# A fused attention and PReLU kernel: relu split by load counters, and the side tasks of a group gathered in one slot

## The chip, the cores and the metric

The kernel runs on one core of a Trainium2 chip. The metric is the device time of one execution in microseconds (us). Five engines work side by side and meet only at semaphores: TensorE (PE, with weight loads listed apart as PEld), VectorE (DVE), ScalarE (ACT), GpSimd (POOL) and SyncE (SP); the last two mostly issue DMAs here. TensorE writes its results into PSUM, which has eight banks of 512 float32 columns over 128 partitions; ACT and DVE read them from there.

## The reference

Four batches of x (12480 rows of 128) go through two attention steps with 32 inducing rows, and the result through a dense layer pair with a PReLU between:

```python
h = mab(I, x)          # 32 rows attend to the 12480 rows of x
a = mab(x, h)          # the 12480 rows of x attend to the 32 rows of h
t = a @ w_in                                   # 128 -> 2048
g = np.maximum(t, 0.0) + alpha * np.minimum(t, 0.0)
out = g @ w_out                                # 2048 -> 128
```

`mab(q, kv)` is softmax(q kv^T / sqrt(128)) kv. The output is 49920 by 128 float32.

## The kernel before

**What is computed how.** The second attention's weights are kept unnormalised: e2 = exp(scores), 32 values for a row of x. Since a @ w_in = (e2 @ h @ w_in) / sum(e2), the kernel makes hW = h @ w_in once for a batch and multiplies e2 with it; the division is done at the very end (it may be moved past the relu, since the sum is positive). PReLU is written as (1 - alpha) relu(t) + alpha t: the first term goes through relu and W1 = (1 - alpha) w_out, the second is linear and folds into a small matrix hA = h @ (w_in diag(alpha) w_out), which is added by "bias matmuls" from e2.

**Tiles.** A group is 512 rows of x (the last group of a batch 192), a supergroup is four groups; a batch has 25 groups. A group is worked in four slots j = 0 to 3. So there are 4 x 25 x 4 = 400 slots, and a flat loop over them (L622 to L630) fixes the order of all engines. A helper `pin` (L56) chains each instruction to the one before it on its engine, so the order written is the order run.

**A slot.** `fill` (L385) issues four matmuls of 32 x 128 weights over 512 columns. The four use different rows of the array, and e2 stands four times over the partitions (`rep`, a replica, made by a trip to DRAM). Each fills one PSUM bank of a ring of six (`bank`, L93). Then each bank is emptied by one relu with a cast to bf16 into the tile gt: on ACT (L405) or on DVE (L408). After the fill come the tasks of this slot, if any, and then `mm2` (L413) of the slot before: 16 matmuls of 128 x 128 that multiply gt with W1 and add into an accumulator (two PSUM banks, taken in turn by groups). After a group's last slot DVE multiplies the accumulator with 1/sum(e2) (`ob`, L441), and POOL issues the DMA to the output.

So in TensorE's order, slot n is: fill n, tasks of n, output matmuls of n - 1. I call the four banks of a fill r = 0 to 3, and write a slot's engines as a word: AADA means that ACT empties banks 0, 1 and 3, and DVE bank 2. As the ring has six banks and a fill takes four, a fill needs the banks that the last fill's r = 0 and 1 used; each task between them takes one bank more and moves that need on by one.

**Who empties a bank.** Before, a small planner decides. It keeps three clocks (TensorE, ACT, DVE; L90) and a time at which each bank comes free; every step adds its estimated time with `spent` (L99), the exponentials, reciprocals and ob among them. In `fill` a bank goes to the engine that would end first (L402, L403). The estimates are in the lines L397 and L398.

**Bias matmuls.** Four matmuls from `rep` with hA (L427 to L434) are added to the accumulator by the `mm2` of j = 0 (for the first group of all by that of j = 3).

**Tasks.** While a batch runs, TensorE also prepares what follows: for the next supergroup the scores (`b_scores`, L306, one exponential on ACT), its replicas by DMA (`b_rep`, L327) and the denominators (`b_den`, L360, sixteen columns and a reciprocal on DVE); for the next batch the load (`a_load`, on POOL's queue), a transposing DMA (`a_xpose`, on SP's), the scores (`a_scores`, with an exponential on ACT and a transposing DMA), the accumulation (`a_accum`, with an addition on DVE), and at its end six steps that make h, hW and hA (`h_sum` to `h_linear`). The lines L592 to L620 place them by group and slot with `at(group, function, j)`; j is 1 where none is given. The supergroup's scores, replicas and denominators stand at j = 3 of three groups in a row, the next batch's steps at j = 1, and the h steps at j = 1 and j = 3.

**Head.** L551 to L574, and the tasks of the first group, prepare batch 0 on TensorE itself, as it has nothing else to do then; POOL scales the weights in eight operations (`w_scale`, L516).

Of the kernel before, what the change touches and what calls it, by code (L numbers as in the profile page):

```python
# [15 lines left out]
P = 128  # L16
NB = 4
GRP = P * NB
NQ = 4
# [5 lines left out]
def kernel(  # L25
# [59 lines left out]
    accs = [psum.tile([P, NB, C], f32, name=f"acc{i}") for i in range(2)]  # L85
    ring_n = [0]

    clk = {"P": 0.0, "A": 0.0, "D": 0.0}  # L90
    free = [0.0] * RING

    def bank():  # L93
        i = ring_n[0] % RING
        ring_n[0] += 1
        clk["P"] = max(clk["P"], free[i])
        return ring[i]

    def spent(e, ns, release=True):  # L99
        clk[e] = max(clk[e], clk["P"] + 100) + ns  # L100
        if release:
            free[(ring_n[0] - 1) % RING] = clk[e] + 100

    def mm(o, lhsT, rhs, start=True, stop=True, **kw):
        return pin(nc.tensor.matmul(o, lhsT, rhs, start=start, stop=stop, **kw))  # L105
# [5 lines left out]
    def new_batch(b):  # L111
        st = Batch()
        st.b = b
        st.xT = xt_pool.tile([C, NS, NQ, GRP], bf16, name="xT", tag="xT")
        st.xTr = xt_pool.tile([C, JR, PR], bf16, name="xTr", tag="xTr")
        st.xn = {}
        st.e1 = {}
        st.e1T = {}
        st.es = work.tile([P, NS + 1], f32, name="es", tag="es")
        st.hacc = work.tile([P, C], f32, name="hacc", tag="hacc")  # L120
        st.e2 = {}
        st.d = {}
        st.rep = {}
        st.rden = {}
        nc.vector.memset(st.es[:], 0.0)
        nc.vector.memset(st.hacc[:], 0.0)
        return st
# [80 lines left out]
    def a_scores(st, u, by_dma=True):  # L208
        ps = bank()
        if u < NS:  # L210
            for q in range(NQ):
                mm(ps[32 * q : 32 * q + 32, :], IT[:], st.xT[:, u, q, :])
            e1 = work.tile([P, GRP], bf16, name="e1", tag="e1")
            pin(nc.scalar.activation(
                out=e1[:], in_=ps[:], func=EXP, scale=scale, accum_out=st.es[:, u : u + 1]
            ))
            if by_dma:
                e1T = work.tile([P, NB, P], bf16, name="e1T", tag="e1T")
                pin(nc.sync.dma_start_transpose(out=e1T[:], in_=e1[:]))
        else:  # L220
            mm(ps[0:M, :REM], IT[:], st.xTr[:].rearrange("c j p -> c (j p)"))
            e1 = e1r
            pin(nc.scalar.activation(
                out=e1[:, :, :PR],
                in_=ps[0:M, :REM].rearrange("m (j p) -> m j p", j=JR),
                func=EXP, scale=scale, accum_out=st.es[0:M, u : u + 1],
            ))
            if by_dma:
                e1T = work.tile([P, JR, M], bf16, name="e1Tr", tag="e1Tr")
                pin(nc.sync.dma_start_transpose(  # L230
                    out=e1T[:], in_=e1[:].rearrange("m j p -> m (j p)")
                ))
        clk["P"] += 320
        spent("A", 680)
        if by_dma:
            st.e1T[u] = e1T
        else:
            st.e1[u] = e1

    def a_accum(st, u):  # L240
        xn = st.xn.pop(u)
        e1T = st.e1T.pop(u)
        ps = bank()
        clk["P"] += 240
        if u < NS:
            for j in range(NB):
                for q in range(NQ):
                    mm(
                        ps[32 * q : 32 * q + 32, :C],
                        e1T[:, j, 32 * q : 32 * q + 32],  # L250
                        xn[:, q, j * C : (j + 1) * C],
                        start=(j == 0), stop=(j == NB - 1),
                    )
            pin(nc.vector.tensor_tensor(
                out=st.hacc[:], in0=ps[:, :C], in1=st.hacc[:], op=ADD
            ))
        else:
            for j in range(JR):
                mm(
                    ps[0:M, :C], e1T[:PR, j, :], xn[:, j, :],  # L260
                    start=(j == 0), stop=(j == JR - 1),
                )
            pin(nc.vector.tensor_tensor(
                out=st.hacc[0:M, :], in0=ps[0:M, :C], in1=st.hacc[0:M, :], op=ADD
            ))

        spent("D", 220)

    def h_sum(st):
        st.et = work.tile([P, 1], f32, name="et", tag="et")  # L270
# [35 lines left out]
    def b_scores(st, s):  # L306
        ps = bank()
        if s < NS:
            for q in range(NQ):
                mm(ps[32 * q : 32 * q + 32, :], st.hT, st.xT[:, s, q, :])  # L310
            e2 = work.tile([P, GRP], bf16, name="e2", tag="e2")
            pin(nc.scalar.activation(out=e2[:], in_=ps[:], func=EXP, scale=scale))
            w = GRP
        else:
            mm(ps[0:M, :REM], st.hT, st.xTr[:].rearrange("c j p -> c (j p)"))
            e2 = work.tile([M, REM], bf16, name="e2r", tag="e2r")
            pin(nc.scalar.activation(out=e2[:], in_=ps[0:M, :REM], func=EXP, scale=scale))
            w = REM

        nq = NQ if s < NS else 1  # L320
        st.d[s] = dram.tile([32 * nq, w], bf16, name="e2d", tag="e2d" if s < NS else "e2dr")
        pin(nc.sync.dma_start(out=st.d[s][:], in_=e2[:]))
        clk["P"] += 320
        spent("A", 490)
        st.e2[s] = e2

    def b_rep(st, s):  # L327
        nq, w = (NQ, GRP) if s < NS else (1, REM)
        rep = rep_pool.tile([P, nq, w], bf16, name="rep", tag="rep" if s < NS else "repr")
        dv = st.d.pop(s)[:].rearrange("(q i) t -> i q t", q=nq)  # L330
        for r in range(4):
            pin(nc.sync.dma_start(out=rep[32 * r : 32 * r + 32], in_=dv))
        for q in range(nq):
            st.rep[s * NQ + q] = rep[:, q, :]


    def b_scores_pe(st, s, q):
# [22 lines left out]
    def b_den(st, s):  # L360
        e2 = st.e2.pop(s)
        ps = bank()
        clk["P"] += 240
        spent("D", 250)
        if s < NS:
            for j in range(NB):
                mm(ps[:, j * NQ : (j + 1) * NQ], e2[:, j * P : (j + 1) * P], pick[:])
# [11 lines left out]
        st.rden[s] = rd  # L379


    def shape_of(g):
        return (P, NB) if g < NS * NQ else (PR, JR)

    def fill(st, g, j):  # L385
# [5 lines left out]
        for r in range(4):  # L391
# [1 line left out]
            mm(  # L393
                ps[:, :w], st.hW[32 * r : 32 * r + 32, j, :], rep[32 * r : 32 * r + 32, :w]
            )
            banks.append((ps, (ring_n[0] - 1) % RING))
        ca, cd = w * 0.75 + 96, w * 1.04 + 68  # L397
        clk["P"] += 100 + w * 0.42  # L398
        ready = clk["P"] + 50
        done = ready  # L400
        for r, (ps, i) in enumerate(banks):
            ta, td = max(clk["A"], ready) + ca, max(clk["D"], ready) + cd  # L402
            if ta <= td:  # L403
                clk["A"] = free[i] = ta
                pin(nc.scalar.activation(out=gt[:, r, :w], in_=ps[:, :w], func=RELU))  # L405
            else:
                clk["D"] = free[i] = td
                pin(nc.vector.tensor_relu(gt[:, r, :w], ps[:, :w]))  # L408
            free[i] += 150
            done = max(done, free[i])  # L410
        return gt, done

    def mm2(st, g, j, gt, done):  # L413
        pp, nb = shape_of(g)
        acc = accs[(st.b * NG + g) % 2]
        clk["P"] = max(clk["P"], done) + 4 * nb * 57
        for r in range(4):
            c = r * NJ + j
            for k in range(nb):
# [2 lines left out]
                    start=(j == 0 and r == 0 and k == 0), stop=False,  # L422
                    skip_group_check=True,
                )


        if j == (NJ - 1 if (st.b, g) == (0, 0) else 0):  # L427
            clk["P"] += nb * 57
            rep = st.rep[g]
            for k in range(nb):  # L430
                mm(
                    acc[:pp, k, :], rep[:, k * pp : (k + 1) * pp], st.hA[:],
                    start=False, stop=True, skip_group_check=True,
                )  # L434
        if j == NJ - 1:
            s, q = divmod(g, NQ)
            rd = st.rden[s]
            rq = rd[:, :, q : q + 1]
# [2 lines left out]
            pin(nc.vector.tensor_tensor(  # L441
                out=ob[:pp, :nb, :], in0=acc[:pp, :nb, :], in1=rbc, op=MULT
            ))
            spent("D", nb * C * 1.04 + 68, release=False)
            t0 = st.b * N + g * GRP
            pin(nc.gpsimd.dma_start(  # L446
                out=out[t0 : t0 + pp * nb, :].rearrange("(p j) c -> p j c", j=nb),
# [144 lines left out]
    for b in range(B):  # L592
        base = b * NG
        for s in range(1, NS + 1):
            g = base + s * NQ - 4
            at(g, lambda b=b, s=s: b_scores(states[b], s), 3)
            at(g + 1, lambda b=b, s=s: b_rep(states[b], s), 3)
            at(g + 2, lambda b=b, s=s: b_den(states[b], s), 3)
        if b + 1 < B:
            n = b + 1  # L600

# [4 lines left out]
            for i, u in enumerate(order):  # L606
                k = base + i * (NG - 13) // NS
                at(k, lambda n=n, u=u: a_load(states[n], u))
                at(k + 3, lambda n=n, u=u: a_xpose(states[n], u))
                at(k + 5, lambda n=n, u=u: a_scores(states[n], u))  # L610
                at(k + 8, lambda n=n, u=u: a_accum(states[n], u))
            k = base + NG - 5
            at(k, lambda n=n: h_sum(states[n]))
            at(k, lambda n=n: h_den(states[n]), 3)
            at(k + 1, lambda n=n: h_transpose(states[n]))
            at(k + 1, lambda n=n: h_weights(states[n]), 3)
            at(k + 2, lambda n=n: b_scores(states[n], 0))
            at(k + 2, lambda n=n: h_linear(states[n]), 3)
            at(k + 3, lambda n=n: b_rep(states[n], 0), 0)
            at(k + 3, lambda n=n: b_den(states[n], 0))  # L620

    prev = None  # L622
    for b, g, j in fills:
        gt, done = fill(states[b], g, j)
        for fn in tasks.pop((b * NG + g, j), []):
            fn()
        if prev is not None:
            mm2(*prev)
        prev = (states[b], g, j, gt, done)
    mm2(*prev)  # L630
    assert not tasks, tasks

# [29 lines left out]
```

## Time and profile before

| what | value |
|---|---|
| median of three runs | 626.52 us (626.24 to 626.53) |
| the profiled execution | 626.24 us, of which the span of the trace is 624.4 us |
| TensorE, matmuls | busy 602.7 us, 97% of the span |
| TensorE, weight loads | busy 446.3 us, 71% |
| DVE, ACT, POOL | busy 84%, 81%, 14% |
| granted TensorE clock | 0.996 of full speed, mean over the span |
| relus of 512 columns | ACT some 0.59 us each, DVE some 0.68 us |

The profile is of one execution. Its span reaches from the first to the last instruction. A line of the timeline gives an instruction's start, its duration, its engine, the line of the kernel, the operation, what it writes and reads, and how often it stands there in a row; in brackets the engine's idle time before it, and what ended it. Matmuls overlap and their ends are modelled, so the sum of their busy times can fill a span in which TensorE could still do more. In the page's name for a tile, ring_81 to ring_86 are the six ring banks, and acc_87 and acc_88 the two accumulators.

### The profile page before, as it was taken

To read this page: it belongs to the slowest core of one execution; us is meant where nothing else is said; L and a number is where in the kernel's file an instruction comes from. 1 tells how busy PE (TensorE), PEld (TensorE's weight loads), DVE (VectorE), ACT (ScalarE), POOL (GpSimd) and SP (SyncE) were. 2 spreads that over 40 slices of the span, in tenths; PEclk is the share of its full clock that TensorE was granted. 3 is DMA by queue.
4 is the path that set the end of the run, shared out by engine and by line. 5 is a ranking of instruction groups with operands and counts; after the bars stand their busy time and mean duration, and the time that the engine had idled before them with its cause. 6 is when DMAs were issued, how large, how long until landed. Compare 5 with 4: busy or idle time off the path is not lost.

```text
span 624.4 us, 21883 instructions
## 1 busy us (share of the span) xinstructions
PE 602.7 (97%) x9198; PEld 446.3 (71%) x9198; DVE 523.5 (84%) x933; ACT 507.4 (81%) x995; POOL 89.4 (14%) x152
## 2 busy tenths in 40 slices
PE   5889999999999999999999999999999999999994
PEld 3557777777777777777777777777777777777773
DVE  4568888888988888888888888888898988898893
ACT  2568888888878888888888888888888888888883
POOL 7131111110111121110111111110111011101110
PEclk9999999999999999999999999999999999999998
DMA  8723889833124488863123588854121222122111
GB/s 138 172 65 71 157 176 180 177 89 94 56 86 116 111 182 168 162 159 89 57 77 90 116 175 163 177 148 121 60 81 58 79 94 76 55 93 95 53 40 41
DMA packets 87394, 68.66 MB, mean 110 GB/s; under 512 B 53200, under 2 KB 80640, under 8 KB 87296
## 3 DMA queue, kind: packets, MB, share of 16 engines
q0 software_dynamic: 21504, 39.92, 26.2%
q1 hardware_dynamic: 65792, 27.35, 19.7%
q8 instruction: 72, 1.18, 0.8%
q14 instruction: 26, 0.21, 0.1%
HBM read 39.94 MB, written 28.62 MB: 110 GB/s over the span
## 4 chain that ended last, share of the span: by engine, by line
PE 58%; issue 32%; POOL 3%; ACT 1%; DVE 1%; POOLq 0%; DVEq 0%; ACTq 0%
PE acc_87 L105 20%; PE acc_88 L105 20%; POOL out_dram L446 3%; PE ring_81 L105 3%; PE ring_83 L105 3%; PE ring_85 L105 3%; PE ring_84 L105 3%; PE ring_86 L105 3%; PE ring_82 L105 3%; DVE gt L408 0%; ACT gt L405 0%; PE acc_88 L528 0%; ACT rep L342 0%; ACT winT L537 0%; POOL xn L136 0%
## 5 line engine op out<-in xcount | busy, mean ns | idle before, releaser
L105 PEld LDWEIGHTS <-gt 128*128 128x128 bf16 x6272 | 352.7, 98 | 83.3 <-issue 78.6
L105 PE MATMUL acc_87<-W_173,gt 128*128 128x128 bf16 (+1 forms) x3136 | 209.8, 220 | 0.0
L105 PE MATMUL acc_88<-W_173,gt 128*128 128x128 bf16 (+1 forms) x3136 | 209.7, 220 | 0.0
L446 POOL DMA_DIRECT2D out_dram<-ob x100 | 54.1, 541 | 509.8 <-DVE ob L441 490.4
L105 PE MATMUL ring_86<-rep,hW 32*128 32x512 bf16 (+1 forms) x274 | 103.5, 378 | 0.5 <-ACT rep L342 0.5
L105 PE MATMUL ring_81<-rep,hW 32*128 32x512 bf16 (+1 forms) x274 | 104.0, 380 | 0.0
L405 ACT ACTIVATE gt<-ring_85 128x512 bf16<-128x512 f32 (+1 forms) x163 | 94.3, 578 | 11.5 <-ACT gt L405 8.4
L405 ACT ACTIVATE gt<-ring_81 128x512 bf16<-128x512 f32 (+1 forms) x150 | 87.3, 582 | 19.3 <-ACT gt L405 15.0
L105 PE MATMUL ring_84<-rep,hW 32*128 32x512 bf16 (+1 forms) x272 | 102.9, 378 | 0.0
L405 ACT ACTIVATE gt<-ring_83 128x512 bf16<-128x512 f32 (+1 forms) x156 | 89.8, 576 | 15.9 <-ACT gt L405 9.0
L105 PE MATMUL ring_83<-rep,hW 32*128 32x512 bf16 (+1 forms) x267 | 100.8, 378 | 0.1
L408 DVE TENSOR_SCALAR gt<-ring_84 128x512 bf16<-128x512 f32 (+1 forms) x138 | 90.6, 656 | 12.2 <-ACT gt L405 5.6
L105 PE MATMUL ring_85<-rep,hW 32*128 32x512 bf16 (+1 forms) x259 | 97.9, 378 | 0.0
L408 DVE TENSOR_SCALAR gt<-ring_81 128x512 bf16<-128x512 f32 x124 | 85.0, 686 | 15.3 <-PE ring_83 L105 8.1
L405 ACT ACTIVATE gt<-ring_82 128x512 bf16<-128x512 f32 x149 | 88.2, 592 | 10.8 <-ACT gt L405 8.3
L405 ACT ACTIVATE gt<-ring_84 128x512 bf16<-128x512 f32 x134 | 80.0, 597 | 20.7 <-ACT gt L405 12.6
L408 DVE TENSOR_SCALAR gt<-ring_86 128x512 bf16<-128x512 f32 (+1 forms) x127 | 83.7, 659 | 15.6 <-PE ring_82 L105 10.1
L105 PE MATMUL ring_82<-rep,hW 32*128 32x512 bf16 (+1 forms) x254 | 96.2, 379 | 0.0
L405 ACT ACTIVATE gt<-ring_86 128x512 bf16<-128x512 f32 x147 | 87.3, 594 | 10.7 <-ACT gt L405 7.0
L408 DVE TENSOR_SCALAR gt<-ring_83 128x512 bf16<-128x512 f32 x111 | 75.9, 684 | 10.7 <-ACT gt L405 5.5
L408 DVE TENSOR_SCALAR gt<-ring_82 128x512 bf16<-128x512 f32 (+1 forms) x105 | 70.1, 667 | 10.5 <-PE ring_84 L105 3.7
L408 DVE TENSOR_SCALAR gt<-ring_85 128x512 bf16<-128x512 f32 x96 | 66.0, 687 | 8.6 <-PE ring_81 L105 3.0
(301 smaller groups left out, 391.2 us busy)
## 6 DMA issues: line engine op xcount, KB each, us to landing
out_dram<-ob POOLq DMA_DIRECT2D x96, 256.0 KB, 2.6
rep<-e2d SPq DMA_DIRECT2D x92, 128.0 KB, 3.4
xn<-in_x_dram POOLq DMA_DIRECT2D x18, 512.0 KB, 6.0
xn<-in_x_dram POOLq DMA_DIRECT2D x12, 256.0 KB, 8.5
w_out_f<-in_moe_w_out_dram POOLq DMA_DIRECT2D x1, 1024.0 KB, 13.6
w_in_b<-in_moe_w_in_dram POOLq DMA_DIRECT2D x1, 512.0 KB, 11.6
out_dram<-ob POOLq DMA_DIRECT2D x4, 96.0 KB, 2.0
xT<-xn SPq DMA_TRANSPOSE x18, 4.6
```

The source lines that it names most:

```text
L105: return pin(nc.tensor.matmul(o, lhsT, rhs, start=start, stop=stop, **kw))
L405: pin(nc.scalar.activation(out=gt[:, r, :w], in_=ps[:, :w], func=RELU))
L408: pin(nc.vector.tensor_relu(gt[:, r, :w], ps[:, :w]))
L446: pin(nc.gpsimd.dma_start(out=out[t0 : t0 + pp * nb, :].rearrange("(p j) c -> p j c", j=nb), in_=ob[:pp, :nb, :],))
```

## The change

The change is named "head pipelined one supergroup deeper, weight scaling in 8 wide gpsimd operations, filler transposes in TensorE gaps, softmax sums folded into the h transpose". The two files agree in the code for all of that: L551 to L574, `w_scale`, `warm` and the h steps themselves stand in both. What differs is this:

- The planner with its clocks is gone. Two counters take its place, one for ACT and one for DVE, of relu time given out so far; ob counts on DVE's, the exponentials, reciprocals and other steps on neither. A bank goes to the engine whose counter would be lower. Bank 3 of j = 0 always goes to ACT.
- The bias matmuls are issued by the `mm2` of j = 3 in all groups.
- All tasks stand at j = 1. A supergroup's scores move from j = 3 of one group to j = 1 of the next; its replica DMAs are issued in the same step as the scores' store to DRAM; its denominators move from j = 3 to j = 1 of the same group.
- The next batch's steps come 2, 4 and 6 groups after the load, in place of 3, 5 and 8, and the h steps begin two groups earlier.

```diff
@@ fill @@
-        ca, cd = w * 0.75 + 96, w * 1.04 + 68
-        clk["P"] += 100 + w * 0.42
-        ready = clk["P"] + 50
...
-            ta, td = max(clk["A"], ready) + ca, max(clk["D"], ready) + cd
-            if ta <= td:
-                clk["A"] = free[i] = ta
...
+        ca, cd = w / 1.2 + 98, w / 0.96 + 75
+        for r in range(4):
+            on_act = load["A"] + ca <= load["D"] + cd
+            if j == 0 and r == 3:
+                on_act = True
+            if on_act:
+                load["A"] += ca
...
+            else:
+                load["D"] += cd
@@ mm2 @@
-        if j == (NJ - 1 if (st.b, g) == (0, 0) else 0):
+        if j == NJ - 1:
             rep = st.rep[g]
             for k in range(nb):
...
-            spent("D", nb * C * 1.04 + 68, release=False)
+            load["D"] += pp * nb / 0.96 * (pp / P) + 75
@@ tasks @@
-            at(g, lambda b=b, s=s: b_scores(states[b], s), 3)
-            at(g + 1, lambda b=b, s=s: b_rep(states[b], s), 3)
-            at(g + 2, lambda b=b, s=s: b_den(states[b], s), 3)
+            at(g + 1, lambda b=b, s=s: b_scores(states[b], s))
+            at(g + 2, lambda b=b, s=s: b_den(states[b], s))
...
-                at(k + 3, lambda n=n, u=u: a_xpose(states[n], u))
-                at(k + 5, lambda n=n, u=u: a_scores(states[n], u))
-                at(k + 8, lambda n=n, u=u: a_accum(states[n], u))
-            k = base + NG - 5
+                at(k + 2, lambda n=n, u=u: a_xpose(states[n], u))
+                at(k + 4, lambda n=n, u=u: a_scores(states[n], u))
+                at(k + 6, lambda n=n, u=u: a_accum(states[n], u))
+            k = base + NG - 7
             at(k, lambda n=n: h_sum(states[n]))
-            at(k, lambda n=n: h_den(states[n]), 3)
-            at(k + 1, lambda n=n: h_transpose(states[n]))
-            at(k + 1, lambda n=n: h_weights(states[n]), 3)
-            at(k + 2, lambda n=n: b_scores(states[n], 0))
-            at(k + 2, lambda n=n: h_linear(states[n]), 3)
-            at(k + 3, lambda n=n: b_rep(states[n], 0), 0)
-            at(k + 3, lambda n=n: b_den(states[n], 0))
+            at(k + 1, lambda n=n: h_den(states[n]))
+            at(k + 2, lambda n=n: h_transpose(states[n]))
+            at(k + 3, lambda n=n: h_weights(states[n]))
+            at(k + 3, lambda n=n: b_scores(states[n], 0))
+            at(k + 3, lambda n=n: h_linear(states[n]))
+            at(k + 4, lambda n=n: b_den(states[n], 0))
```

More of the change, by code (lines that the diff above doesn't have):

```diff
@@ L86 @@
     ring_n = [0]
-    clk = {"P": 0.0, "A": 0.0, "D": 0.0}
-    free = [0.0] * RING
     def bank():
-        i = ring_n[0] % RING
+        t = ring[ring_n[0] % RING]
         ring_n[0] += 1
[L96 to L102, printed above, removed]
+        return t
     def mm(o, lhsT, rhs, start=True, stop=True, **kw):
@@ L121, in new_batch @@
         st.e2 = {}
-        st.d = {}
         st.rep = {}
@@ L232, in a_scores @@
                 ))
-        clk["P"] += 320
-        spent("A", 680)
         if by_dma:
@@ L243, in a_accum @@
         ps = bank()
-        clk["P"] += 240
         if u < NS:
@@ L265, in a_accum @@
             ))
-        spent("D", 220)
     def h_sum(st):
@@ L320, in b_scores @@
         nq = NQ if s < NS else 1
[L321 to L328, printed above, removed]
+        d = dram.tile([32 * nq, w], bf16, name="e2d", tag="e2d" if s < NS else "e2dr")
+        pin(nc.sync.dma_start(out=d[:], in_=e2[:]))
         rep = rep_pool.tile([P, nq, w], bf16, name="rep", tag="rep" if s < NS else "repr")
-        dv = st.d.pop(s)[:].rearrange("(q i) t -> i q t", q=nq)
+        dv = d[:].rearrange("(q i) t -> i q t", q=nq)
         for r in range(4):
@@ L334, in b_rep @@
             st.rep[s * NQ + q] = rep[:, q, :]
+        st.e2[s] = e2
     def b_scores_pe(st, s, q):
@@ L362, in b_den @@
         ps = bank()
-        clk["P"] += 240
-        spent("D", 250)
         if s < NS:
@@ L379, in b_den @@
         st.rden[s] = rd
+    load = {"A": 0.0, "D": 0.0}
     def shape_of(g):
@@ L395, in fill, with mm2 @@
             )
-            banks.append((ps, (ring_n[0] - 1) % RING))
-        ca, cd = w * 0.75 + 96, w * 1.04 + 68
-        clk["P"] += 100 + w * 0.42
-        ready = clk["P"] + 50
-        done = ready
-        for r, (ps, i) in enumerate(banks):
-            ta, td = max(clk["A"], ready) + ca, max(clk["D"], ready) + cd
-            if ta <= td:
-                clk["A"] = free[i] = ta
-                pin(nc.scalar.activation(out=gt[:, r, :w], in_=ps[:, :w], func=RELU))
-            else:
[L407 to L413, printed above, removed]
+            banks.append(ps)
+        ca, cd = w / 1.2 + 98, w / 0.96 + 75
[5 more added lines that the diff above has]
+                load["A"] += ca
+                pin(nc.scalar.activation(out=gt[:, r, :w], in_=banks[r][:, :w], func=RELU))
+            else:
+                load["D"] += cd
+                pin(nc.vector.tensor_relu(gt[:, r, :w], banks[r][:, :w]))
+        return gt
+    def mm2(st, g, j, gt):
         pp, nb = shape_of(g)
         acc = accs[(st.b * NG + g) % 2]
-        clk["P"] = max(clk["P"], done) + 4 * nb * 57
         for r in range(4):
@@ L424, in mm2 @@
                 )
-        if j == (NJ - 1 if (st.b, g) == (0, 0) else 0):
-            clk["P"] += nb * 57
+        if j == NJ - 1:
             rep = st.rep[g]
@@ L434, in mm2 @@
                 )
-        if j == NJ - 1:
             s, q = divmod(g, NQ)
@@ L608 @@
                 at(k, lambda n=n, u=u: a_load(states[n], u))
-                at(k + 3, lambda n=n, u=u: a_xpose(states[n], u))
-                at(k + 5, lambda n=n, u=u: a_scores(states[n], u))
-                at(k + 8, lambda n=n, u=u: a_accum(states[n], u))
-            k = base + NG - 5
+                at(k + 2, lambda n=n, u=u: a_xpose(states[n], u))
+                at(k + 4, lambda n=n, u=u: a_scores(states[n], u))
+                at(k + 6, lambda n=n, u=u: a_accum(states[n], u))
+            k = base + NG - 7
             at(k, lambda n=n: h_sum(states[n]))
-            at(k, lambda n=n: h_den(states[n]), 3)
-            at(k + 1, lambda n=n: h_transpose(states[n]))
-            at(k + 1, lambda n=n: h_weights(states[n]), 3)
-            at(k + 2, lambda n=n: b_scores(states[n], 0))
-            at(k + 2, lambda n=n: h_linear(states[n]), 3)
-            at(k + 3, lambda n=n: b_rep(states[n], 0), 0)
-            at(k + 3, lambda n=n: b_den(states[n], 0))
+            at(k + 1, lambda n=n: h_den(states[n]))
[4 more added lines that the diff above has]
+            at(k + 4, lambda n=n: b_den(states[n], 0))
     prev = None
     for b, g, j in fills:
-        gt, done = fill(states[b], g, j)
+        gt = fill(states[b], g, j)
         for fn in tasks.pop((b * NG + g, j), []):
@@ L628 @@
             mm2(*prev)
-        prev = (states[b], g, j, gt, done)
+        prev = (states[b], g, j, gt)
     mm2(*prev)
```

## The prediction

> **What bounds the kernel now.** I read the page first: busy shares, then the chain that ended last.
>
> ```profile
> PE 602.7 (97%) x9198; PEld 446.3 (71%) x9198; DVE 523.5 (84%) x933; ACT 507.4 (81%) x995; POOL 89.4 (14%) x152
> ...
> PE 58%; issue 32%; POOL 3%; ACT 1%; DVE 1%; POOLq 0%; DVEq 0%; ACTq 0%
> ```
>
> The chain is TensorE (58%) and TensorE that waits for nothing the profile shows (32%); ACT and DVE, which empty its PSUM banks, hold 1% each. The table of windows, for the stretch in which the 400 slots run (columns: length, then busy us and instruction counts of PE, PEld, DVE, ACT, POOL, then clock and DMA), says the same:
>
> ```profile
> 45.00:610.00 565.00, 564.93 (x8657) 419.13 (x8654) 495.30 (x846) 481.44 (x945) 67.38 (x118) 1.00 0.47 111
> ```
>
> Since ends of matmuls are modelled, I trust starts only: the distance between two fills' first weight loads (LDWEIGHTS <-hW) in the timeline. A slot without a task takes 1.32 to 1.33 us; with the four bias matmuls 1.55 (so +0.22); with those and a scores or accumulate task 1.88 (+0.33); with a denominator task 1.43 (+0.10). These numbers return for every slot of a kind: TensorE runs at its own pace, and that pace is the floor. It is left in two kinds of slot, and both show how this kernel loses time. Here is a denominator slot (j = 3), from the timeline:
>
> ```profile
> 75.02 0.10 PEld L105 LDWEIGHTS <-hW 32*128 32x128 bf16 x4
> ...
> 75.35 0.25 PE L105 MATMUL ring_83<-pick,e_1127 128*128 128x4 bf16 x4
> ...
> 75.49 0.60 ACT L405 ACTIVATE gt<-ring_85 128x512 bf16<-128x512 f32 x1 [0.27 <-ACT gt L405]
> 75.53 0.69 DVE L408 TENSOR_SCALAR gt<-ring_86 128x512 bf16<-128x512 f32 x1
> 75.98 0.59 ACT L405 ACTIVATE gt<-ring_81 128x512 bf16<-128x512 f32 x1
> 76.14 0.68 DVE L408 TENSOR_SCALAR gt<-ring_82 128x512 bf16<-128x512 f32 x1
> 76.44 0.10 PEld L105 LDWEIGHTS <-hW 32*128 32x128 bf16 x4
> 76.45 0.38 PE L105 MATMUL ring_84<-rep,hW 32*128 32x512 bf16 x1
> ...
> 76.63 0.37 PE L105 MATMUL ring_81<-rep,hW 32*128 32x512 bf16 x1
> ```
>
> The task took a bank (ring_83), so the next fill needs ring_81, the third bank of this one, in place of only the first two. ACT frees it at 75.98 + 0.59 = 76.57; the matmul starts 0.06 later, 0.18 after its sisters, and the slot that should take 1.33 takes 1.48: 19 such slots, 0.15 each. The other kind is the slot after the output multiply (ob), where two banks in a row are ACT's:
>
> ```profile
> 60.30 0.68 DVE L408 TENSOR_SCALAR gt<-ring_84 128x512 bf16<-128x512 f32 x1
> 60.50 0.10 PEld L105 LDWEIGHTS <-hW 32*128 32x128 bf16 x4
> ...
> 60.89 0.68 DVE L441 TENSOR_TENSOR ob<-acc_88,rd 128x512 f32<-128x512 f32 x1
> 60.97 0.60 ACT L405 ACTIVATE gt<-ring_85 128x512 bf16<-128x512 f32 x1 [0.24 <-ACT gt L405]
> 61.47 0.59 ACT L405 ACTIVATE gt<-ring_86 128x512 bf16<-128x512 f32 x1
> 61.49 0.68 DVE L408 TENSOR_SCALAR gt<-ring_81 128x512 bf16<-128x512 f32 x1
> ...
> 62.11 0.37 PE L105 MATMUL ring_86<-rep,hW 32*128 32x512 bf16 x1
> ```
>
> ob holds DVE from 60.89, so DVE gets one bank of this slot, the third, which nobody needs soon. ACT's second release lands 1.61 after the fill's start; the slot is 1.55 long because the bias matmuls are in it (j = 0's matmuls run one slot late), and the loss is 0.03 (38 slots of 1.35 to 1.37). So before loses 19 x 0.15 + 38 x 0.03 = 4.0 us in banks.
>
> **The rule I use.** Times from a fill's start: first relu 0.47; ACT's next 0.50 later, DVE's 0.61 later; a relu lasts 0.60 on ACT, 0.68 on DVE; hand-over 0.05. Releases: first 1.12 (ACT) or 1.20 (DVE), ACT's second 1.62, third 2.12, DVE's second 1.81. A fill without tasks before it needs the first two banks of the last fill, with one task the first three, with two all four. A wait costs release minus slot length minus 0.03 (1.61 - 1.43 - 0.03 = 0.15, as measured). Behind a waiting fill stand TensorE's 16 output matmuls, and ob behind those: a wait is paid in full.
>
> **What does not move.** The words of the change name the head, the weight scaling, filler transposes and the folded sums; all four stand alike in both files, so they cost nothing. TensorE's instructions are equal in number and kind. DVE loses 12 relus to ACT (899 becomes 911 of 1600), neither being the bound: nothing. The replica DMAs now follow the scores' store at once on SP's queue, where they wait for it and hold back the transposes behind them. They did so before too, for SP waits on data and not on slots (a store at 40.94, its first copy at 42.68); only their place among the transposes changes. Store and copies take 1.7 + 3.4 us (the latter the page's median to landing); the transposes have two groups (11 us) before a matmul needs them, the replica 2.7 groups (15 us): nothing. If that cover went, TensorE would wait up to a landing, 3.4 us, at each of 24 supergroups, 80 us; with three times the time in hand I leave that out of the range.
>
> **What moves: the bias matmuls go from j = 0 to j = 3.** Their 0.22 now lengthens the slot ahead of ob's slot, not ob's slot itself. So group slot 0 is 1.55 long, and DVE's order there is relus, ob, relus of slot 1. The accumulator is ready 0.11 after slot 1's fill starts (ob at 43.60 after a fill at 43.49); with two DVE relus before it, ob starts at 0.47 + 2 x 0.61 - 1.55 = 0.13. The next DVE relu starts 0.60 later, at 0.73, and frees its bank at 0.73 + 0.68 + 0.05 = 1.46; DVE's second at 2.07. The old planner knew this and gave slot 1 the pattern AADA (94 of 100). The counters know only totals: slot 1 is ADAD, DADA, DAAD or ADAA in 82 cases of the 99 after the first group, and DVE owns one of the first two banks.
>
> **What moves: all tasks go to j = 1**, the very slot in which DVE is late. Prices by slot 1's tasks (pattern counts are read off the changed program's order of instructions):
> - none, 33 slots, next fill wanted at 1.36: DVE first 24 x 0.10 = 2.4; AADA or AAAD 8 x (1.61 - 1.36) = 2.0; one DDAA 0.71. Sum 5.1.
> - one scores task, 24 slots, third bank wanted at 1.69: only DADA waits, 9 x (2.07 - 1.69) = 3.4. Six slots with an h step alike: 2 x 0.4 = 0.8.
> - denominator alone, 9 slots, third bank at 1.46: DADA 5 x 0.61 = 3.1; the rest 4 x 0.15 = 0.6. Sum 3.7.
> - several tasks, 27 slots: two denominators 3 x 0.53; denominator and accumulate 3 x 0.29; the four-task slot 3 x 0.24 (its cast on DVE); three tasks 9 x 0.12 (a reciprocal behind the relus); scores and accumulate 9 x 0.06. Sum 4.8.
>
> **Elsewhere.** Planned blindly, 13 slots at j = 2 and 3 have AADA without cover: 13 x 0.25 = 3.3; two DDAA at j = 0: 0.5. All new waits: 5.1 + 3.4 + 0.8 + 3.7 + 4.8 + 3.8 = 21.6. The old ones (4.0) go, the net is +17.6. Each wait frees ACT and DVE for a moment, so nothing accumulates: two DVE relus are 1.22 against 1.33.
>
> No row of before shows DVE's late release holding a fill with a task. From below: 0, if the matmul that waits is hidden; if that were so for all, before's 4.0 would be gained. From above: the full second DVE release everywhere, 2.07 - 1.36 = 0.71 in the plain slots. The value taken, by the denominator slots' own 0.15, is nearest to what was measured.
>
> **Two rules of the Trainium skill.** In the window from 35 to 40 us TensorE was busy 3.18 of 5.00 us and the granted clock stayed 1.00. The page "TensorE: Matmul & The Clock Gate" (section "A second HAM failure mode: psum-queue depth-cycling") says that small idle gaps between matmul groups that cycle through banks make the clock swing to half; by it, an estimate, each tenth of the 570 us body at half clock would add 57 us. The row speaks against it, and I add nothing. Second, PEld is busy 419 of 565 us (74%). "Perfetto Trace Analysis" (section "Identifying the Most-Contended Engine") judges TensorE's headroom by weight loads, not by matmul busy time; by it a quarter of each slot, 0.34 us, would be free and swallow most of these waits, leaving an estimated 2 us. But 1.43 followed by 1.48 says that no such headroom exists.
>
> **Rivals.**
> - Waits run one release deeper (DVE later than I think, ob starting late): plain slots 33 x 0.71, scores 30 x 0.38, denominators 9 x 0.61, the rest 9: 23 + 11 + 5 + 9 - 4 = +44, 670 us. Against: DVE is busy 88% only. Chance 0.12.
> - Half hidden: the fill's first two matmuls go ahead, plain waits vanish, and only the 0.38 and 0.61 remain: about +7, 633 us. For: 0.10 is near my reading error. Chance 0.11.
> - Faster: nothing new waits, as ob starts early enough to release DVE's first bank before 1.36 (0.10 earlier than computed) and second banks are never needed; before's 4.0 are gained: 622.2 us. Against: ob cannot start before the accumulator is ready at 0.11. Chance 0.04.
> - The change does nothing, since only the head is named and the head is equal: 626.2. Against: the slot plan differs. Chance 0.03.
>
> **Numbers.** The sum is made on the profiled execution, 626.24 us (span 624.4 and 1.84 around it), 0.28 below the median. 626.24 + 17.6 = 643.8, say 644 (chance 0.70, its own range 636 to 656). 634 to 660 also takes half of each slower rival: 0.81. Under 0.2% (1.25 us) a measurement here cannot tell from no change: faster 0.04, same 0.03, slower 0.93.
>
> **What would show it.** Gaps between fills after slot 1 of 1.43 or more where before had 1.33; waits of fill matmuls for DVE's relu; slot 0 at 1.55, slot 1 at 1.33 or 1.66; the reciprocal's DADA slots worst; clock still 1.00; ACT and DVE busy within 10 us of before. Wrong if slots after j = 1 keep 1.33, or if waits come from a DMA.

## The result and the profile after

The changed kernel takes 660.65 us (median of four runs, 652.09 to 662.89) against 626.38 us. It is 1.050 times as long, with a 95% interval of 1.040 to 1.060; this ratio leaves out the longest run, which lies over 1.5% above the shortest and counts as slow (the medians of all runs give 1.055). On the forecast's basis (626.24 us) the ratio makes 657.7: the forecast direction, at the upper edge of the range (634 to 660), with two of the four runs, and the median itself, beyond it. The spread is part of the result: the kernel before stays within 0.4 us. The profiled execution is the longest of the four, 662.89 us with a span of 661.1, so 36.65 us over the profiled execution of before.

The page of the changed kernel, busy shares and chain:

```profile
PE 621.9 (94%) x9198; PEld 453.4 (69%) x9198; DVE 519.5 (79%) x921; ACT 513.5 (78%) x1007; POOL 89.4 (14%) x152
...
PE 45%; issue 32%; DMA 8%; POOL 3%; ACT 2%; DVE 1%; SPq 0%; POOLq 0%; DVEq 0%
```

TensorE executes the same 9198 matmuls and is idle for the first time in the body; ACT and DVE have about the work they had. New in the chain is DMA with 8%, a releaser that the kernel before did not have there. The wait list names it (engine and line, then what was waited for: total us, times, longest):

```profile
PEld L94 <- DMA xT<-xn: 13.3, 6, 3.4
```

**The waits that were forecast.** The timeline of a group with a denominator task at j = 1 and the pattern DADA:

```profile
520.41 0.10 PEld L94 LDWEIGHTS <-hW 32*128 32x128 bf16 x4
...
520.52 0.69 DVE L411 TENSOR_TENSOR ob<-acc_87,rd 128x512 f32<-128x512 f32 x1 [0.45 <-PE acc_87 L94]
...
521.13 0.68 DVE L385 TENSOR_SCALAR gt<-ring_82 128x512 bf16<-128x512 f32 x1
...
521.73 0.68 DVE L385 TENSOR_SCALAR gt<-ring_84 128x512 bf16<-128x512 f32 x1
521.84 0.12 PEld L94 LDWEIGHTS <-hW 32*128 32x128 bf16 x4
...
522.46 0.37 PE L94 MATMUL ring_84<-rep,hW 32*128 32x512 bf16 x1 [0.21 <-DVE gt L385]
```

ob begins 0.11 us after the fill, DVE's relus follow it at 0.72 and 1.32, the second ends at 522.41, and the last matmul of the fill that began at 521.84 starts at 522.46. The next fill comes 1.92 us after that one where it would be 1.33: 0.59, and the forecast said 0.61. Note that the busy column hides this: the other three matmuls of the fill keep PE "busy" meanwhile.

**A wait that was not forecast, on banks.** A slot with three tasks (denominator, accumulation, scores):

```profile
414.78 0.38 PE L94 MATMUL ring_81<-rep,hW 32*128 32x512 bf16 x1
...
415.50 0.68 DVE L385 TENSOR_SCALAR gt<-ring_81 128x512 bf16<-128x512 f32 x1
...
416.23 0.40 PE L94 MATMUL ring_81<-xT,IT 128*32 128x512 bf16 x4 [0.49 <-DVE gt L385]
```

The tasks took ring_85, ring_86 and then ring_81, the first bank of the fill of this very slot, which DVE frees only at 416.18. The slot is 2.78 us long where its instructions need 2.09.

**A wait that was not forecast, on DMA.** The scores of the next batch wait for the transposed x:

```profile
398.55 0.41 PE L94 MATMUL ring_86<-xn,e1T 128*32 128x128 bf16 x16
...
401.53 0.10 PEld L94 LDWEIGHTS <-IT 128*32 128x32 bf16 x4 [2.75 <-DMA xT<-xn]
```

and the table of windows around it (columns as in the prediction; the number before the last two is the granted clock) shows what follows:

```profile
396.00:398.90 2.90, 2.90 (x58) 2.12 (x55) 2.86 (x5) 2.23 (x5) 0.00 (x0) 1.00 1.36 140
398.90:401.50 2.60, 0.05 (x4) 0.00 (x0) 0.93 (x3) 1.37 (x3) 1.30 (x2) 1.00 0.79 221
402.60:406.00 3.40, 3.40 (x30) 2.21 (x28) 1.29 (x2) 1.16 (x3) 0.00 (x0) 0.52 1.58 168
```

TensorE stands for 2.6 us; about a microsecond after it resumes, the granted clock is 0.52 for 3.4 us, in which 30 matmuls pass where 58 passed in 2.9 us. Such a stretch came four times in the execution.

### The profile page after: what moved, and what is told of

Same layout as the page of the kernel before. It is cut to its first block, busy times and chain, and to the rows that moved or that the text cites. A ratio compares the mean times of both kernels' runs of the same rounds, so it can differ in the third digit from the quotient of the medians.

```text
span 661.1 us, 21831 instructions
## 1 busy us (share of the span) xinstructions
PE 621.9 (94%) x9198; PEld 453.4 (69%) x9198; DVE 519.5 (79%) x921; ACT 513.5 (78%) x1007; POOL 89.4 (14%) x152
## 4 chain that ended last, share of the span: by engine, by line
PE 45%; issue 32%; DMA 8%; POOL 3%; ACT 2%; DVE 1%; SPq 0%; POOLq 0%; DVEq 0%
PE acc_87 L94 16%; PE acc_88 L94 15%; DMA xT<-xn 8%; POOL out_dram L416 3%; PE ring_81 L94 3%; PE ring_82 L94 2%; PE ring_83 L94 2%; PE ring_85 L94 2%; PE ring_86 L94 2%; PE ring_84 L94 2%; ACT gt L382 2%; DVE gt L385 1%; SPq L207 0%; DVE ob L411 0%; ACT winT L507 0%
## 5 line engine op out<-in xcount | busy, mean ns | idle before, releaser
L94 PEld LDWEIGHTS <-gt 128*128 128x128 bf16 x6272 | 357.0, 99 | 101.2 <-issue 99.0
L94 PE MATMUL acc_87<-W_173,gt 128*128 128x128 bf16 (+1 forms) x3136 | 213.6, 222 | 0.0
L94 PE MATMUL acc_88<-W_173,gt 128*128 128x128 bf16 (+1 forms) x3136 | 211.0, 220 | 0.0
L382 ACT ACTIVATE gt<-ring_83 128x512 bf16<-128x512 f32 (+1 forms) x154 | 90.8, 589 | 23.0 <-ACT gt L382 8.1
L382 ACT ACTIVATE gt<-ring_81 128x512 bf16<-128x512 f32 (+1 forms) x152 | 89.7, 590 | 22.4 <-ACT gt L382 11.2
L382 ACT ACTIVATE gt<-ring_85 128x512 bf16<-128x512 f32 (+1 forms) x157 | 92.1, 586 | 18.4 <-ACT gt L382 10.7
L382 ACT ACTIVATE gt<-ring_84 128x512 bf16<-128x512 f32 (+1 forms) x155 | 90.9, 587 | 16.0 <-PE ring_81 L94 7.9
L382 ACT ACTIVATE gt<-ring_86 128x512 bf16<-128x512 f32 x147 | 86.5, 589 | 14.6 <-ACT gt L382 5.7
L382 ACT ACTIVATE gt<-ring_82 128x512 bf16<-128x512 f32 (+1 forms) x146 | 86.2, 590 | 15.0 <-ACT gt L382 6.8
L385 DVE TENSOR_SCALAR gt<-ring_82 128x512 bf16<-128x512 f32 (+1 forms) x116 | 78.0, 672 | 19.7 <-PE ring_85 L94 12.6
L385 DVE TENSOR_SCALAR gt<-ring_86 128x512 bf16<-128x512 f32 (+1 forms) x115 | 77.2, 671 | 17.3 <-PE ring_83 L94 9.7
L385 DVE TENSOR_SCALAR gt<-ring_84 128x512 bf16<-128x512 f32 (+1 forms) x121 | 81.1, 671 | 9.3 <-PE ring_81 L94 3.3
L385 DVE TENSOR_SCALAR gt<-ring_83 128x512 bf16<-128x512 f32 (+1 forms) x117 | 77.8, 665 | 12.3 <-PE ring_85 L94 4.2
L385 DVE TENSOR_SCALAR gt<-ring_85 128x512 bf16<-128x512 f32 (+1 forms) x116 | 78.1, 674 | 9.1 <-PE ring_81 L94 4.1
L385 DVE TENSOR_SCALAR gt<-ring_81 128x512 bf16<-128x512 f32 (+1 forms) x104 | 69.7, 670 | 16.3 <-PE ring_83 L94 8.3
## 6 DMA issues: line engine op xcount, KB each, us to landing
w_in_b<-in_moe_w_in_dram POOLq DMA_DIRECT2D x1, 512.0 KB, 12.1
```

Of the source, the lines that this page charges most:

```text
L382: pin(nc.scalar.activation(out=gt[:, r, :w], in_=banks[r][:, :w], func=RELU))
L385: pin(nc.vector.tensor_relu(gt[:, r, :w], banks[r][:, :w]))
```

## The experiments

Times are medians; "over before" is against the runs of before on the same chip (626.3 to 626.5). The prediction had dismissed the DMAs, so the first question was what makes xT late. In the trace of the changed kernel the transposing DMA landed after 7.3 us (median), in that of before after 4.6. The view of the tile xT has these lines, before first:

```profile
DMA to landing us min/median/max: 4.3/4.6/6.1
```

```profile
DMA to landing us min/median/max: 4.3/7.3/12.1
```

The timelines of POOL and of SP show the neighbours (POOL first, the load of the next x):

```profile
387.61 0.76 POOL L124 DMA_DIRECT2D xn<-in_x_dram  x1
```

```profile
388.22 1.20 SPq L207 DMA_TRANSPOSE e1T<-e_7256  x1
389.52 6.58 SPq L138 DMA_TRANSPOSE xT<-xn  x1
402.70 1.19 SPq L207 DMA_TRANSPOSE e1T<-e_7498  x1
```

The transpose issued at 389.52 landed at 401.5, the end of TensorE's wait above. A load of 512 KB began 1.9 us before it. In the kernel before, counted from a batch's first group, loads stand in even groups and transposes in odd ones (3 groups after a load); with 2 groups in place of 3 a transpose shares its slot with the load of the next supergroup. The last transpose of a batch has no load beside it. In the changed kernel these three landed after 4.3, 4.3 and 4.4 us, the other fifteen after 4.4 to 12.1 (median 7.8). The load that a transpose itself needs had landed at least 5.4 us before each was issued, so the shorter distance to it is not what makes the transposes late.

**e1: loads one group earlier.**

```diff
-                at(k, lambda n=n, u=u: a_load(states[n], u))
+                at(max(k - 1, base), lambda n=n, u=u: a_load(states[n], u))
```

> The changed kernel with each load of the next batch issued one group earlier (the first load of a batch stays); nothing on TensorE, ACT or DVE moves. Theory A, collision: the transposing DMA of one supergroup runs beside the load of the next, issued in the same slot, and that is why it lands after 7.3 us (median) and up to 12.1 in place of 4.6; with the load a group ahead the landing goes back to 4 to 6 us, TensorE's waits for xT (some 15 us) and the half clock after them (some 3 us) go, and the time falls to 642 to 647 us, with little spread. Rival B, queue place: the transpose is late because it stands behind the e1T transpose on SP's queue, which waits for an exponential; the load changes nothing of that, and the time stays between 652 and 662 us. Rival C, banks alone: xT is late only where bank waits moved things; time within 3 us of the changed kernel.

Measured: 645.08 us (645.00 to 645.15), 1.030 times before (1.028 to 1.032). No wait for xT is left, and the landing times of the transposes, from the view of the tile xT (minimum, median, maximum), are those of before:

```profile
DMA to landing us min/median/max: 4.3/4.5/6.3
```

So 15.6 us of the change's 34.3 by the medians (7.0 to 17.8 by the single run), and all of its spread, come from the place of the loads relative to the transposes. Rivals B and C fall.

**e2: transposes earlier in SP's order, loads left where they are.**

```diff
-                at(k + 2, lambda n=n, u=u: a_xpose(states[n], u))
+                at(k + 1, lambda n=n, u=u: a_xpose(states[n], u), 3)
```

> The changed kernel with each transposing DMA of x placed three slots earlier in the written order (j = 3 of the group before), so that it stands ahead of the e1T transpose on SP's queue; nothing on TensorE, ACT or DVE moves, and the loads stay where they are. Theory A, collision: the transpose now starts before the load of its slot is issued, so it lands in some 5 us and, even if not, has over one group more time; the waits for xT go: 642 to 647 us. Rival B, queue place: the same time, but by the queue; A and B part in the trace, by the landing time of the transposes (A: back to 4 to 6 us; B: still 7 us or more beside loads, only started earlier). Rival C, banks alone: 652 to 662 us.

Measured: 649.36 us, but 645.0 to 657.9 from run to run. The transposes are still slow (median 6.3, up to 12.8 us), and so are some loads of 512 KB (up to 12.7 us, against 7.9 before); in the profiled execution TensorE no longer waits for xT, but twice, 5.3 us in all, for e1T, the transposed exponentials, and the mean clock falls to 0.989. The queue's order decides which transfer is late; it does not take the collision away. The expected time of A was met in the best run only.

**e10: the same collision made in the kernel before, with one edit.**

```diff
-                at(k, lambda n=n, u=u: a_load(states[n], u))
+                at(k + 1, lambda n=n, u=u: a_load(states[n], u))
```

> The kernel before with one edit: each load of the next batch one group later, so that it is issued in the same group and slot as a transposing DMA of x, as in the change; split, bias matmuls and every other place are those of before. Theory A, collision: the transposes land late, TensorE waits at the next batch's scores and the clock halves after it, with no other part of the change present: 640 to 655 us, spread over some us from run to run. Rival (a load beside a transpose costs nothing here unless the change's other parts stand beside it): 626 to 628 us.

Measured: 643.98 us (641.85 to 645.99), 1.028 times before (1.025 to 1.031), with nothing else of the change present. The view of the tile xT has the same wait (us, times) and slow landings:

```profile
  DMA xT<-xn: 14.4, 8
...
DMA to landing us min/median/max: 4.3/9.0/11.4
```

The three transposes that have no load beside them landed after 4.3 to 5.4 us. Both directions together show that a load beside a transpose is the cause; which resource the two share was not tested.

**e5: the places of the change alone**, with the planner and the bias matmuls of before (the diff is the third hunk of the change, with `b_rep` called in the same step as `b_scores`).

> The kernel before with only the places of tasks and DMAs of the change (planner and bias matmuls of before). The planner's pattern at j = 1 is AADA in 94 of 100 groups. By the rule of releases the slots lose little to late releases of the slot before, and the denominators' 0.15 at j = 3 go (-3); the slots with three tasks and more take a bank of their own fill and wait for it (9 x 0.37 + 3 x 0.5 = +5): 628 us without DMA waits. Theory A, collision: the places put load and transpose in one slot, so waits for xT and the half clock after them come back, 7 to 18 us as in the changed kernel, with a spread between runs: 635 to 645 us. Rival (the waits for xT need the changed split too): 627 to 630 us.

Measured: 654.51 us (651.43 to 655.77), 1.044 times before (1.042 to 1.047) and 28 us over it: theory A's mechanism, but 10 us more than its range. TensorE stood 18.4 us for xT (7 times) against 12.3 (6 times) in the changed kernel. Three of its four stretches at half clock lasted 6.8 us, where those of the changed kernel lasted 3.4. A TensorE with fewer bank waits passes its two groups sooner and so reaches the late transfer sooner; that would explain the longer waits, but no run isolates it.

**e9: the same with loads one group earlier** (e1's edit on e5).

> The kernel before with the places of the change (654.5 us) and each load one group earlier. Theory A, collision of load and transpose: the waits for xT and the half clock go, and what the places cost by banks alone is left, some +2 us over before: 627 to 631 us. Rival (the shorter steps from load to use, 2, 4 and 6 groups, are what hurts, whatever runs beside the transposes): 640 us or more.

Measured: 628.45 us (628.12 to 629.68), 1.004 times before (1.002 to 1.005). Without the collision the places cost 2 us; the shorter steps from the transpose to its use hurt nothing by themselves (a transpose stands 3 groups after its load again).

**e3: the split by counters alone.** In `fill` the counters choose the engine, with bank 3 of j = 0 forced to ACT; the clocks still run but decide nothing:

```diff
+        na, nd = w / 1.2 + 98, w / 0.96 + 75
...
-            if ta <= td:
+            on_act = load["A"] + na <= load["D"] + nd
+            if j == 0 and r == 3:
+                on_act = True
+            if on_act:
+                load["A"] += na
...
+                load["D"] += nd
```

> The kernel before with only the split by counters (bank 3 of j = 0 forced to ACT included); bias matmuls and tasks stay where they were. By the rule of releases: slot 0 is 1.33 long, so ob comes 0.1 to 0.4 us after slot 1's fill, DVE's first release at 1.44 to 1.69 against 1.58; 37 slots lose 0.11, 13 uncovered AADA lose 0.25, DADA in scores and denominator slots at j = 3 lose 0.12 and 0.35. Sum some +9 to +13 us over the kernel before: 635 to 640 us. Rival (the split alone is harmless, as the two engines keep their totals): 626 to 629 us. No waits for xT in either.

Measured: 637.85 us (637.70 to 639.33), 1.019 times before (1.017 to 1.021), 11.5 us over it, inside the range worked out by releases; no wait for xT. DVE and ACT do about the same total work as before: the order in which banks come free is the cost, not the load.

**e4: the bias matmuls at j = 3 alone.**

```diff
-        if j == (NJ - 1 if (st.b, g) == (0, 0) else 0):
+        if j == NJ - 1:
```

> The kernel before with only the bias matmuls moved to j = 3; the planner's clocks know it, and its pattern at j = 1 stays AADA in 94 of 100 groups. By the rule of releases ACT's second release at 1.61 now meets a fill wanted at 1.36 in the 50 or so slots at j = 1 that have no task: 50 x 0.25, so +10 to +12 us: 636 to 639 us, with slots after j = 1 of 1.58 to 1.60. Rival (the planner moves the cover with the bias matmuls, or the cover was not needed): 626 to 628 us.

Measured: 633.40 us (633.25 to 633.54), 1.011 times before (1.010 to 1.013), 7.1 us over it. The expectation was wrong in its premise: the planner does not keep AADA at j = 1, it takes ADAA in 92 of 100 groups, as the order of the built program shows. Then DVE's first release is the one waited for, at 0.09 to 0.15 and not 0.25: the 44 slots that follow one without a task (41 of them after ADAA) take 3.7 us more than before. So the rival was half right: the planner softens the loss of the cover, but cannot avoid it. In the trace another 2.9 us stand in 18 slots at j = 3, which take 1.48 or 1.49 us in place of 1.33; why those lose time was not followed up.

**e8: the bias matmuls back at j = 0, in the changed kernel with early loads.** The edit is e4's backwards (with the output step kept at j = 3).

> The changed kernel with loads one group earlier (645.1 us) and the bias matmuls back at j = 0, the split by counters and the tasks as in the change. By the rule of releases slot 1 is 0.22 longer, so its fills' successors are wanted later: plain slots lose 0.0 to 0.11 in place of 0.10, AADA 0.03 in place of 0.25, one scores task with DADA 0.14 in place of 0.38; nine AADA or DDAA slots at j = 0 lose 0.25 to 0.45 anew. Sum -4 to -7 us: 638 to 641 us. Rival (with blind counters the place of the bias matmuls is indifferent): 644 to 646 us.

Measured: 639.89 us (639.60 to 640.23), 5.2 below e1, as worked out.

**e6: denominators at j = 3, in the changed kernel with early loads.**

```diff
-            at(g + 2, lambda b=b, s=s: b_den(states[b], s))
+            at(g + 2, lambda b=b, s=s: b_den(states[b], s), 3)
```

> The changed kernel with loads one group earlier, as in the first of these runs (645.1 us), and a supergroup's denominators at j = 3 of their group in place of j = 1. Theory: a third task in one slot takes the first bank of the same slot's fill and waits for its relu, which costs 0.36 to 0.9 us in each of nine slots (4.9 us); split, that goes, and denominators at j = 3 cost about what they cost alone at j = 1 (4.5 against 4.1 us): 639 to 642 us. Rival (three tasks cost what their instructions cost, wherever they stand): 644 to 646 us.

Measured: 642.27 us (642.21 to 642.77), 2.8 below e1. The direction is the theory's, and the rival's 644 to 646 is out, but the gain is a little smaller than the 3 to 6 expected. The waits on a slot's own bank are real (the line above shows one), and splitting three tasks takes them away (13 of the 15 slots with accumulation and scores now take the 1.88 us that they need), at the price of denominator waits at j = 3: the 20 slots that follow them take 1.57 to 1.94 us, where 1.55 is needed.

**e7: denominators into the idle accumulator, in the kernel before.** If the 0.15 us after a denominator is a matter of banks, it goes when the denominator takes none:

```diff
-    def b_den(st, s):
+    def b_den(st, s, idle):
         e2 = st.e2.pop(s)
-        ps = bank()
+        ps = accs[idle % 2][:].rearrange("p k c -> p (k c)")
...
-            at(g + 2, lambda b=b, s=s: b_den(states[b], s), 3)
+            at(g + 2, lambda b=b, s=s, i=g + 3: b_den(states[b], s, i), 3)
...
-            at(k + 3, lambda n=n: b_den(states[n], 0))
+            at(k + 3, lambda n=n, i=k + 4: b_den(states[n], 0, i), 3)
```

> The kernel before with the denominators' matmuls written into the accumulator that is idle at that time (the next group's) in place of a ring bank; the first denominators of a batch move from j = 1 to j = 3 for that. Nothing else moves. By the rule of releases the fill after a denominator then needs only two banks of the last fill, and the 0.15 in each of 19 slots goes: 623.0 to 624.0 us, a ratio of about 0.995. Rival (the wait is the denominators' own drain, not the bank): 626 us, no change.

Measured: 622.32 us (621.87 to 622.64), 0.993 times before (0.992 to 0.995): faster than both kernels, and than before by 4.2 us, where 19 x 0.15 = 2.9 was expected. The rival falls: in the trace all 20 slots after such a denominator take 1.33 us, which is 3.4 us less than before (one of them had taken 1.76). The rest, mostly in the last groups of a batch, was not followed up.

## Why the prediction was right, and where it was wrong

The direction was right, and so was the mechanism of the bank waits: they were forecast at +17.6 us, and the changed kernel without the collision (e1) costs +18.7. But the whole change costs 34.3. On the forecast's basis 657.7 is 13.9 above its centre of 643.8, and for these 13.9 it had no mechanism. That the result still lies inside the range is luck: the range was stretched to 660 for waits one release deeper, which did not come to pass. One of its own signs of being wrong came true, waits from a DMA, and the clock did not stay at 1.00 as it expected.

The distances between fills in the trace of the changed kernel, each less what its instructions take, give the forecast's terms one by one (us):

| term of the prediction | forecast | measured |
|---|---|---|
| after j = 1, no task | 5.1 | 4.5 |
| after one scores task or an h step | 4.2 | 4.5 |
| after a denominator alone | 3.7 | 3.6 |
| slots with several tasks | 4.8 | 9.1, of which 6.0 inside the slot |
| elsewhere (j = 2, 3, 0) | 3.8 | 2.9 |
| all bank waits | 21.6 | 24.6 |
| net of before's 4.0 | +17.6 | +20.6 here; +18.7 in e1 |
| TensorE standing for xT | 0 | 12.3 |
| half clock after it, 4 x 3.4 us | 0 | 6.8 (worked out: half of each stretch) |

The last two terms and the 20.6 make 39.7, with e1's 18.7 they make 37.8, against 36.65 for the profiled execution. So the parts add up to 1 to 3 us too much; where they overlap was not traced.

- **The bound and the rule of releases held.** TensorE's own pace is the floor, and a fill's wait is release minus slot length minus 0.03: plain slots with one of DVE's banks among the first two 0.09 to 0.12 in 19 of 23 (forecast 0.10), AADA without cover 0.25 to 0.27 (0.25), scores with DADA 0.36 (0.38), denominators with DADA 0.59 (0.61).
- **None of the rivals came about.** Banks alone would have made 645, as e1 shows, 1.3 us from the forecast; what took the time to 660 was in no rival.
- **"What does not move" held for the head** (the first fill starts at 30.3 us against 30.2) and for the totals of ACT and DVE.
- **It failed for the DMAs.** The step said that the transposes have two groups (11 us) before a matmul needs them and cost nothing. It set only the 1.7 + 3.4 us of store and copies against that, and took these from a schedule in which loads and transposes stand in different groups; a transpose's own landing, 4.6 us before, is not in it. It looked at SP's queue and not at what POOL starts in the same slot. The two groups from transpose to matmul are the same in both kernels; what the steps of 2, 4 and 6 groups do is to put a load and a transpose into one slot, where the transpose lands after 7.3 us and up to 12.1. In the case shown it was issued at 389.52, TensorE wanted its data at 398.9, and it landed at 401.5. e1 and e10 show it both ways: -15.6 us and +17.6 us with one line. The step left that term out of the range; its own bound for it (a landing of 3.4 us at each of 24) was of the right kind, and too lightly dropped.
- **It missed the third task.** The need was counted for the next fill only; from three banks on a task needs a bank of its own slot's fill (6.0 us).
- **On the clock it was right and incomplete.** Waits of a few tenths leave the granted clock alone: e8 and e6, full of them, show 0.995. So the rule on cycling through banks did not apply. But the waits for DMA did halve the clock. The page "TensorE: Matmul & The Clock Gate" of the Trainium skill (section "HAM oscillation — how this bites in real kernels") says that a wait for DMA longer than about 3.4 us between bursts of matmuls makes the next burst start at half clock. In the changed kernel four of five waits with 2.1 us and more of idle weight loads did it (3.42, 2.75, 2.36 and 2.21 us; one of 2.10 did not), and each cost a stretch of 3.4 us. So gaps shorter than the page's figure are enough in this trace; the stretch is as long as the window that the page gives. But the length of the gap does not decide alone. In e10 a gap of 3.36 us left the clock full, and one of 2.19 us was followed by half clock (each gap, then the window after it):

```profile
283.71 0.10 PEld L105 LDWEIGHTS <-IT 128*32 128x32 bf16 x4 [3.36 <-DMA xT<-xn]
...
283.70:287.10 3.40, 3.39 (x51) 2.50 (x52) 1.33 (x3) 1.79 (x5) 0.00 (x0) 1.00 0.41 105
```

```profile
424.63 0.10 PEld L105 LDWEIGHTS <-IT 128*32 128x32 bf16 x4 [2.19 <-DMA xT<-xn]
...
425.49:428.90 3.41, 3.41 (x34) 2.78 (x31) 1.29 (x2) 1.36 (x4) 0.00 (x0) 0.50 1.00 102
```

- **The rule on weight loads** would have left 2 us of bank waits; e1 shows 18.7. Slack in LDWEIGHTS busy time was no slack here.
- **The terms do not add, because of the collision.** Split +11.5, bias matmuls +7.1 and places +28.1 make 46.7; the whole change costs 34.3. With the places freed of the collision (+2.0 in e9) the three make 20.6, near e1's 18.7. The collision itself is worth 26.1 us beside the old split (e5 less e9) and 15.6 beside the new one. That a kernel which waits for banks reaches a late DMA later, and waits there less, would explain it; it was not tested.

## What to carry to other kernels

Where the bound engine runs without a gap, a scheduling change is priced by when each buffer comes free and which instruction wants it next, slot by slot; equal totals on the emptying engines say nothing. Before calling a DMA hidden, list what every queue starts in the same stretch after the change: a landing time read from the old schedule holds only for the old neighbours. A stall of 2 to 3 us on TensorE can cost nearly as much again in clock: four of five did here, at some 1.7 us each (an estimate: half of a stretch of 3.4 us).

## What the runs showed of the hardware

A load of 512 KB beside a transposing DMA of the same tile size makes the transpose late: with no other edit the transposes' median landing went from 4.6 to 9.0 us in e10. For the loads of 512 KB the runs show less: their median went from 6.0 to 6.5 us and the longest from 7.9 to 9.4, but e7, which has no such collision, has a median of 6.9. The clock's reaction to a stall was sharp in the changed kernel: full, then 0.52 over a window of 3.4 us, then full again, four times alike; in e5 three of four such stretches lasted 6.8 us.
